# The five last pieces of the output, each stored as two sets of partitions

## The chip, the cores and the metric

The kernel runs on one core of one Trainium2 chip. A core has the engines TensorE (PE; its weight loads are listed apart, as PEld), VectorE (DVE), ScalarE (ACT), GpSimd (POOL) and SyncE (SP), and 16 DMA engines that move data between the chip's memory (HBM) and the core's on-chip memory (SBUF, 128 partitions). An instruction of SP, ACT or POOL can issue a DMA; the DMA engines then carry it out as packets, while the issuing engine goes on. The metric is the time of one execution on the device in microseconds (us), as the median of several runs. A profile is taken of one more execution; its span runs from the first to the last instruction of the program.

## The reference

Four batches of 6400 tokens with 256 channels. Attention runs over the channels (a 256 x 256 matrix for each batch), and its output goes through a mixture of eight low-rank adapters, of which each token takes two:

```
qn = q / (norm(q, axis=tokens) + 1e-6);  kn likewise        # q, k, v: 4 x 6400 x 256, f32
s  = kn^T @ qn / tau                                        # 4 x 256 x 256
a  = softmax(s, last axis)
x  = v @ a                                                  # 25600 x 256 rows
logits = x @ w_gate                                         # 8 experts
w  = softmax(the two largest logits of each row)
out = x + sum over the two experts e: w_e * ((x @ A[e]) @ B[e])   # A: 256x16, B: 16x256
```

The output is 25600 x 256 in f32, 26.2 MB.

## The kernel before, in words

**Layout.** Partition p of a batch holds the 50 tokens 50p to 50p+49 (`"(b p c) d -> b p c d"`), so a "chunk" c is one token of each of the 128 partitions: 128 rows of 256 numbers. Two chunks make a pair; there are 25 pairs in a batch (`NPAIR`) and 100 in all (`NPT`). In the output a pair is, on each partition, one stretch of 2 x 256 f32 numbers, that is 2 KB, and 256 KB over the 128 partitions.

**Stages.** For the first batch q and k are loaded, and their Gram matrix and the norms of their columns accumulate on TensorE. From then on each batch's v is worked on while the next batch's q and k come in. A pair goes through these steps: `transposes` (v turned round), `logits` and `gating` (per group of pairs), `z_gz` (the adapters' first half, times the gate), `y_mm` (v @ a), `gz_t` (transpose), `delta` (the adapters' second half added to y in the same accumulator, then the copy of the result to the SBUF tile `ys`, and its store).

**Groups and stores.** The pairs of a batch are bundled in groups of five that share one `ys` tile of 128 x 10 chunks (10 KB on a partition, 1280 KB in all); the last batch ends with groups of five, five, five, five, three and two. A group of five is stored whole by a DMA that ACT issues (`send`, line 666). The five last pairs of all (`u >= NPT - GRP` in `delta`, line 654: u = 95 to 99, the groups of three and two) are not stored by groups: each pair is stored by a DMA of its own that SP issues as soon as its copy to `ys` (line 651) is done (line 656). So the program has 19 stores from ACT and five from SP. SP does nothing else but to issue five loads at the very start (lines 206 to 213) and to wait at the end until all DMAs have landed (the waits stand under the last line of the launch, L886). Loads of q, k and v come from POOL (lines 181, 182, 185).

**What sets the order.** The order of the instructions is written by a planner in the Python code: it keeps an estimated clock for each engine and for the transfers and picks the next step that is ready. The five stores from SP aren't entered in these clocks. Each engine carries out its own instructions in the order of the program and waits at semaphores.

**Completion semaphores.** The framework below the kernel gives each DMA that SP or ACT issues one of eight completion semaphores, by turns, in the order of the program: the operands of these issues in the trace name 108, 109, 110, 111, 113, 116, 117, 118 and then 108 again, without a break from the first load to the last store. A DMA's landing counts that semaphore up, and in the trace the issuing engine waits, ahead of each of the five stores from SP, for the semaphore that the store is going to use, that is for the landing of the DMA eight places earlier in this sequence. The sequence ends as follows: the three last stores from ACT hold 116, 117 and 118, the five stores from SP hold 108, 109, 110, 111 and 113.

Of the kernel before, what the change touches and what calls it, by code (L numbers as in the profile page):

```python
# [16 lines left out]
def kernel(  # L17
# [16 lines left out]
    nc = tc.nc  # L34
# [11 lines left out]
    NPT = B * NPAIR  # L46
    GRP = 5
# [22 lines left out]
    def run(e, us, *deps):  # L70
        clock[e] = max([clock[e]] + [d + (0.0 if e == "pe" else 0.05) for d in deps]) + us
        return clock[e] + (0.2 if e == "pe" else 0.0)
# [35 lines left out]
    out_v = out.rearrange("(b p c) d -> b p c d", b=B, p=P)  # L108
# [334 lines left out]
    for b in range(B):  # L443
        f = 0
        for n in [5, 5, 5, 5, 3, 2] if b == B - 1 else [GRP] * (NPAIR // GRP):
            g = {"b": b, "f": b * NPAIR + f, "n": n, "ready": False}
            groups += [g] * n
            f += n
    pr = {}
    unsent = []  # L450
    free_from = [None]
# [185 lines left out]
    def delta(u):  # L637
        r, gr = pr[u], groups[u]
        for sc in range(2):
            nc.tensor.matmul(r["y"][:, sc, :], r["gzT"][:, sc, :], ball_sb, start=False,  # L640
                             stop=(sc == 1), skip_group_check=True)
        if "ys" not in gr:
            gr["ys"] = y_pool.tile([P, 2 * GRP, C], FP32, tag="ys", name="ys")
            ys_used.append(gr)
        dst = gr["ys"][:, r["w"]:r["w"] + 2, :]
        t_end = run("pe", 0.215)
        if clock["dve"] + 1.0 < clock["act"]:
            nc.vector.tensor_copy(dst, r["y"])
            r["y_end"] = run("dve", 0.69, t_end)
        else:  # L650
            nc.scalar.copy(dst, r["y"])  # L651
            r["y_end"] = run("act", 0.58, t_end)
        gr["y_end"] = r["y_end"]
        if u >= NPT - GRP:
            c0 = 2 * (u % NPAIR)
            nc.sync.dma_start(out_v[gr["b"], :, c0:c0 + 2, :], dst)
        elif u == gr["f"] + gr["n"] - 1:
            unsent.append(gr)

# [50 lines left out]
    while nd < NPT:  # L710
# [17 lines left out]
        while si["b"] < B and len(squared) < 4:  # L728
            b, c = si["b"], si["c"]
# [19 lines left out]
        if nl < len(order_g) and nt >= order_g[nl]["f"] + order_g[nl]["n"]:  # L749
            gr = order_g[nl]  # L750
# [3 lines left out]
        if nd < ny:  # L754
            r = pr[nd]
            gr = groups[nd]
# [33 lines left out]
        if gi["b"] < B:  # L790
            b, c = gi["b"], gi["c"]
# [31 lines left out]
        elif what == "delta":  # L823
            delta(nd)
            nd += 1
        elif what == "gzt":
            gz_t(ng)
            zuse_end[zuse_of[ng]] = pr[ng]["gzT_end"]
            ng += 1
        elif what == "y":  # L830
            y_mm(ny)
            ny += 1
        elif what == "z":
            if free_from[0] is None and chain_at[B - 1] >= 3:
                free_from[0] = nz
            zuse_of[nz] = zbank(nz)[0]
            z_gz(nz)
            nz += 1
        elif what == "t":
            transposes(nt)  # L840
            nt += 1
        elif what == "norm":
            norm()
        elif what == "gram":
            gram(gi["b"], gi["c"])
            gram(gi["b"], gi["c"] + 1)
            gi["c"] += 2
            if gi["c"] == NC:
                gi["b"], gi["c"] = gi["b"] + 1, 0
# [41 lines left out]
```

## Time and profile before

| what | value |
|---|---|
| time, median of 3 runs | 256.69 us (256.43 to 259.15) |
| time of the profiled execution | 256.61 us |
| its span, first to last instruction | 254.8 us |
| share of the span that engines are busy | PE 85%, PEld 76%, DVE 69%, ACT 63%, POOL 14% |
| mean granted TensorE clock | 0.969 of full speed |
| stores from ACT | 19 of 1280 KB, median 11.3 us from issue to landing |
| stores from SP | 5 of 256 KB, median 6.7 us from issue to landing |

The 1.8 us by which the execution is longer than its span lie before the first and after the last instruction. In a timeline, a row gives the start, the duration, the engine (SPq and ACTq are the sequencers that issue DMAs), the line of the kernel, the operation, and output<-input. In a table by windows, each row gives the stretch and its length, then busy time and number of instructions for each engine, the granted clock, the mean busy share of the 16 DMA engines (1.00: all 16 all the time) and the rate in GB/s. The list of DMA issues gives for each kind its number, its size and the median time from the issue to the landing of its last part.

### The profile page before, as it was taken

The page shows a single profiled execution, that of the slowest core. Times are in us where ns is not written, and L with a number is a line of the kernel's source. Part 1 is how long each engine was busy: PE and PEld are TensorE (multiplying, and loading weights), DVE is VectorE, ACT ScalarE, POOL GpSimd, SP SyncE. Part 2 cuts the span into 40 slices and gives each one's busy share as a digit, 9 for nine tenths or more (in the row PEclk, how much of TensorE's full clock was granted, in tenths as well). Part 3 has the DMA queues.
Part 4 walks back from the last instruction along what each step waited for, and adds up shares of the span by engine and source line. Part 5 has one row for each costly group of instructions (what it writes and reads, how often), then busy time and mean ns, then how long its engine had stood idle before and what let it go on. Part 6 is the DMA issues. An engine that isn't in the chain of part 4 may idle for free.

```text
span 254.8 us, 7166 instructions
## 1 busy us (share of the span) xinstructions
PE 216.9 (85%) x2972; PEld 193.0 (76%) x2972; DVE 174.9 (69%) x639; ACT 160.8 (63%) x289; POOL 36.3 (14%) x74
## 2 busy tenths in 40 slices
PE   1966996799999998999999887969877979999960
PEld 1755984599899997879888777868676869898840
DVE  1040006797979887688889878898657988887840
ACT  2000005688969889359799795958748847775550
POOL 7312341111121210200121010101000000000000
PEclk9998897999999999799999999999999999999995
DMA  7999999999999999999999999999999999999994
GB/s 212 226 214 212 209 216 212 216 215 212 216 214 213 217 213 213 216 214 227 302 257 272 279 252 299 228 316 238 292 241 287 264 265 330 394 425 422 428 411 193
DMA packets 13712, 66.79 MB, mean 262 GB/s; under 512 B 1648, under 2 KB 2416, under 8 KB 11248
## 3 DMA queue, kind: packets, MB, share of 16 engines
q0 software_dynamic: 9504, 38.80, 75.2%
q10 hardware_dynamic: 2736, 24.90, 23.6%
q1 hardware_dynamic: 1440, 2.63, 3.1%
q8 instruction: 23, 0.38, 0.5%
q14 instruction: 9, 0.07, 0.1%
HBM read 78.91 MB, written 26.21 MB: 413 GB/s over the span
## 4 chain that ended last, share of the span: by engine, by line
PE 50%; DMA 32%; DVE 6%; ACT 5%; issue 2%; POOL 1%; ACTq 1%; POOLq 0%
DMA qk<-in_k_dram 32%; PE y_ps L616 12%; PE acc L305 11%; PE vT_ps L467 6%; PE y_ps L640 6%; PE zg L599 5%; PE zg L625 3%; PE lp L495 3%; PE nrm L319 2%; ACT ys L651 2%; ACT sq L286 1%; PE nrm L330 1%; ACT vT L477 1%; POOL qk L181 1%; PE nrm L374 1%
## 5 line engine op out<-in xcount | busy, mean ns | idle before, releaser
L286 ACT ACTIVATE sq<-qk 128x1024 bf16<-128x1024 bf16 x69 | 69.6, 1056 | 4.9 <-DVE s L294 3.2
L305 PE MATMUL acc<-qk 128*128 128x256 bf16 x400 | 62.6, 284 | 4.3 <-DMA qk<-in_k_dram 4.3
L651 ACT COPY ys<-y_ps 128x512 f32<-128x512 f32 x94 | 53.4, 587 | 17.0 <-PE y_ps L640 16.6
L616 PE MATMUL y_ps<-a_bf,vT 128*128 128x256 bf16 x400 | 59.2, 272 | 2.4 <-ACT ys L651 2.2
L603 DVE TENSOR_TENSOR gz<-zg,gate 128x256 bf16<-128x256 f32 x100 | 41.2, 420 | 7.9 <-PE zg L599 7.1
L305 PEld LDWEIGHTS <-qk 128*128 128x128 bf16 x400 | 36.4, 101 | 8.1 <-DMA qk<-in_k_dram 4.8
L467 PE MATMUL vT_ps<-ident,vt 128*128 128x128 bf16 x400 | 36.6, 224 | 5.6 <-ACT vT L477 1.9
L616 PEld LDWEIGHTS <-vT 128*128 128x128 bf16 x400 | 35.9, 97 | 6.8 <-issue 3.5
L640 PE MATMUL y_ps<-ball_sb,gzT 128*128 128x256 bf16 x200 | 36.4, 273 | 1.7 <-ACT gzT L630 1.0
L599 PE MATMUL zg<-wa_sb,vT 128*128 128x128 bf16 x400 | 37.4, 219 | 0.0
L467 PEld LDWEIGHTS <-vt 128*128 128x128 bf16 x400 | 27.9, 101 | 8.7 <-issue 5.1
L294 DVE TENSOR_TENSOR s<-sq 128x512 bf16<-128x512 bf16 x75 | 30.4, 418 | 1.6 <-ACT sq L286 1.2
L319 PE MATMUL nrm<-qk 128*128 128x128 bf16 x200 | 22.3, 237 | 10.5 <-DVE qk L226 5.0
L477 ACT COPY vT<-vT_ps 128x512 bf16<-128x512 bf16 x38 | 22.2, 588 | 13.4 <-PE vT_ps L467 13.0
L480 DVE COPY vT<-vT_ps 128x512 bf16<-128x512 bf16 x62 | 25.1, 420 | 7.0 <-PE vT_ps L467 6.4
L599 PEld LDWEIGHTS <-vT 128*128 128x128 bf16 x400 | 27.4, 98 | 1.0 <-issue 0.2
L319 PEld LDWEIGHTS <-qk 128*128 128x128 bf16 x200 | 17.1, 107 | 13.4 <-DVE qk L226 5.0
L625 PE MATMUL zg<-ident,gz 128*128 128x128 bf16 x200 | 26.2, 219 | 0.8 <-DVE gz L603 0.8
L633 DVE COPY gzT<-zg 128x256 bf16<-128x256 bf16 x68 | 19.3, 288 | 7.2 <-PE zg L625 6.6
L181 POOL DMA_DIRECT2D qk<-in_q_dram x23 | 12.5, 543 | 63.9 <-ACT sq L286 25.4
L347 ACT ACTIVATE lnn<-ss 128x4 f32<-128x4 f32 x1 | 0.2, 205 | 32.5 <-DVE ss L346 32.5
L640 PEld LDWEIGHTS <-gzT 128*128 128x128 bf16 x200 | 16.6, 97 | 4.5 <-ACT gzT L630 1.7
(70 smaller groups left out, 227.2 us busy)
## 6 DMA issues: line engine op xcount, KB each, us to landing
out_dram<-ys ACTq DMA_DIRECT2D x19, 1280.0 KB, 11.3
vt<-in_v_dram POOLq DMA_DIRECT2D x20, 640.0 KB, 26.1
qk<-in_q_dram POOLq DMA_DIRECT2D x17, 640.0 KB, 24.0
qk<-in_k_dram POOLq DMA_DIRECT2D x17, 640.0 KB, 24.5
out_dram<-ys SPq DMA_DIRECT2D x5, 256.0 KB, 6.7
qk<-in_q_dram POOLq DMA_DIRECT2D x3, 320.0 KB, 19.7
qk<-in_k_dram POOLq DMA_DIRECT2D x3, 320.0 KB, 19.3
stage<-in_q_dram SPq DMA_DIRECT2D x1, 512.0 KB, 3.8
```

Of the source, the lines that this page charges most:

```text
L286: nc.scalar.activation(sq, x, ACT.Square)
L294: nc.vector.tensor_tensor(out=s2, in0=sq[:, :, 0, :], in1=sq[:, :, 1, :], op=OP.add)
L305: nc.tensor.matmul(acc[b][:, ic, :], t[:, 1, o, ic * P:(ic + 1) * P], t[:, 0, o, :], start=(c == 0 and ic == 0), stop=(c == NC - 1), skip_ ...
L319: nc.tensor.matmul(nrm[b][:, j * P:(j + 1) * P], x, x, start=(c == 0 and j == 0), stop=(c == NC - 1), skip_group_check=True)
L467: nc.tensor.matmul(pt[:, ic, sc * P:(sc + 1) * P], vt[:, o + sc, ic * P:(ic + 1) * P], ident, is_transpose=True, start=(i == 0), stop=(i = ...
L480: nc.vector.tensor_copy(dst, src)
L599: nc.tensor.matmul(z[:, sc, :], r["vT"][:, ic, sc, :], st[b]["wa"][:, ic, E:E + ER], start=(sc == 0 and ic == 0), stop=(sc == 1 and ic == ...
L603: nc.vector.tensor_tensor(out=gz.rearrange("p c (e r) -> p c e r", e=E), in0=z.rearrange("p c (e r) -> p c e r", e=E), in1=gr["gate"][:, r ...
L616: nc.tensor.matmul(y[:, sc, :], r["vT"][:, ic, sc, :], st[b]["a"][:, ic, :], start=(sc == 0 and ic == 0), stop=False, skip_group_check=True)
L625: nc.tensor.matmul(gt[:, sc, :], r["gz"][:, sc, :], ident, is_transpose=True, start=(sc == 0), stop=(sc == 1))
L640: nc.tensor.matmul(r["y"][:, sc, :], r["gzT"][:, sc, :], ball_sb, start=False, stop=(sc == 1), skip_group_check=True)
L651: nc.scalar.copy(dst, r["y"])
```

## The change

The store of each of the five last pairs, one DMA of 128 partitions before, is issued as two DMAs one after the other from SP for the first four pairs: partitions 0 to 119 and 120 to 127; 0 to 103 and 104 to 127; 0 to 87 and 88 to 127; 0 to 125 and 126 to 127. The fifth pair is stored by one DMA of 128 partitions as before. The bytes on each partition (2 KB) and their places in the output stay as they are. SP issues nine DMAs in place of five.

```diff
@@ -446,6 +446,7 @@
             g = {"b": b, "f": b * NPAIR + f, "n": n, "ready": False}
             groups += [g] * n
             f += n
+    ROWS = [[120, 128], [104, 128], [88, 128], [126, 128], [128]]
     pr = {}
     unsent = []
     free_from = [None]
@@ -653,7 +654,10 @@
         gr["y_end"] = r["y_end"]
         if u >= NPT - GRP:
             c0 = 2 * (u % NPAIR)
-            nc.sync.dma_start(out_v[gr["b"], :, c0:c0 + 2, :], dst)
+            lo = 0
+            for hi in ROWS[u - NPT + GRP]:
+                nc.sync.dma_start(out_v[gr["b"], lo:hi, c0:c0 + 2, :], dst[lo:hi])
+                lo = hi
         elif u == gr["f"] + gr["n"] - 1:
             unsent.append(gr)
```

## The prediction

> **What bounds the kernel now.** I read the page's chain of work first, then what goes on behind its end. The chain, in order of time, closes with the copy of the last pair:
>
> ```profile
> 247.43 0.59 ACT ys L651
> ```
>
> It ends at 248.02, but the span has 254.8 us. No compute engine works in the last 6.8 us; what runs are the DMA engines. The table by windows shows them (the column before the last is their mean busy share):
>
> ```profile
> 248.00:249.00 1.00, 0.00 (x0) 0.00 (x0) 0.00 (x0) 0.02 (x1) 0.00 (x0) 1.00 1.00 399
> 249.00:249.50 0.50, 0.00 (x0) 0.00 (x0) 0.00 (x0) 0.00 (x0) 0.00 (x0) 0.67 1.03 410
> 249.50:250.00 0.50, 0.00 (x0) 0.00 (x0) 0.00 (x0) 0.00 (x0) 0.00 (x0) 0.50 0.81 324
> 250.00:250.50 0.50, 0.00 (x0) 0.00 (x0) 0.00 (x0) 0.00 (x0) 0.00 (x0) 0.50 0.65 250
> 250.50:251.00 0.50, 0.00 (x0) 0.00 (x0) 0.00 (x0) 0.00 (x0) 0.00 (x0) 0.50 0.66 254
> 251.00:251.50 0.50, 0.00 (x0) 0.00 (x0) 0.00 (x0) 0.00 (x0) 0.00 (x0) 0.50 0.68 262
> 251.50:252.00 0.50, 0.00 (x0) 0.00 (x0) 0.00 (x0) 0.00 (x0) 0.00 (x0) 0.50 0.54 209
> 252.00:252.50 0.50, 0.00 (x0) 0.00 (x0) 0.00 (x0) 0.00 (x0) 0.00 (x0) 0.50 0.46 176
> 252.50:253.00 0.50, 0.00 (x0) 0.00 (x0) 0.00 (x0) 0.00 (x0) 0.00 (x0) 0.50 0.30 115
> 253.00:253.50 0.50, 0.00 (x0) 0.00 (x0) 0.00 (x0) 0.00 (x0) 0.00 (x0) 0.50 0.09 33
> ```
>
> A share times 16 is a number of engines: all 16 until 249.5, then 10 to 11 until 251.5 (0.65 to 0.68), 7 at 252.0 to 252.5, 5 after that, 1 or 2 at the end. So five or six engines are done by 250, and ten are **late**, the last of them by 3.5 us. From 248 on the shares add up to 1.00 + 0.5 x 5.22 = 3.61 us of all 16: spread evenly, the packets would end at 251.6. In fact the last two move after 253.3, as the queue's line of the window from 253.3 to the end has it:
>
> ```profile
> q1 hardware_dynamic: 2, 0.00, 0.4%
> ```
>
> So even a perfect spread is worth 253.4 - 251.6 = 1.8 us, 0.7% of the time.
>
> The timeline of ACT's two last stores and SP's five, and the list of issues for each of them in the same order, give issue and landing:
>
> ```profile
> 236.17 0.34 ACTq L666 DMA_DIRECT2D out_dram<-ys  x1
> 242.25 0.34 ACTq L666 DMA_DIRECT2D out_dram<-ys  x1
> 244.20 0.35 SPq L656 DMA_DIRECT2D out_dram<-ys  x1
> 244.69 1.01 SPq L656 DMA_DIRECT2D out_dram<-ys  x1
> 245.79 1.00 SPq L656 DMA_DIRECT2D out_dram<-ys  x1
> 246.89 0.58 SPq L656 DMA_DIRECT2D out_dram<-ys  x1
> 248.04 0.33 SPq L656 DMA_DIRECT2D out_dram<-ys  x1
> ```
>
> ```profile
> out_dram<-ys ACTq DMA_DIRECT2D x1, 1280.0 KB, 11.3
> out_dram<-ys ACTq DMA_DIRECT2D x1, 1280.0 KB, 8.7
> out_dram<-ys SPq DMA_DIRECT2D x1, 256.0 KB, 7.0
> out_dram<-ys SPq DMA_DIRECT2D x1, 256.0 KB, 7.1
> out_dram<-ys SPq DMA_DIRECT2D x1, 256.0 KB, 6.7
> out_dram<-ys SPq DMA_DIRECT2D x1, 256.0 KB, 6.2
> out_dram<-ys SPq DMA_DIRECT2D x1, 256.0 KB, 5.7
> ```
>
> The last store from ACT lands at 242.25 + 8.7 = 250.95, SP's first at 251.2, its third at 252.5, its fourth at 253.1, its fifth at 248.04 + 5.7 = 253.74, about 0.35 after the last packets. They land some 0.6 us apart although they are issued 0.5 to 1.2 apart: on the latest engine they stand in line. The span ends 1.1 us after the last landing.
>
> **The change part by part.** It removes four stores of 128 partitions, adds eight of fewer, all on SP's queue, and moves the fifth pair's store behind them. Nothing before 244.2 us can change: SP issues nothing there, and no other engine waits for these stores. Three things have to be costed.
>
> *Packets on the late engines.* The queue's line for the window from 240 us to the end:
>
> ```profile
> q1 hardware_dynamic: 720, 1.31, 21.4%
> ```
>
> 720 packets for five stores are 144 each: 128 rows of 2 KB and 16 completions, so eight rows on each of 16 engines, 40 in all. 21.4% of 16 engines over the 16 us asked for are 54.8 us, or 0.086 us for a row with its share of the completions; eight rows take 0.69 us, near the 0.6 by which the landings follow each other. What a set of 120 partitions does no row shows. By the nearest one (eight rows to an engine) 120 rows use 15 engines, 104 use 13, 88 use 11; 126 rows can go nine to an engine over 14. Then up to five engines are relieved, and the rest take 8 + 8 + 8 + 9 + 8 = 41 rows and their part of the small sets (8, 24, 40 and 2 rows): spread over all 16 that is 74 / 16 = 4.6 rows more, packed onto the same 8 to 12 engines up to 1 + 2 + 4 + 1 = 8. So a busiest engine has 46 to 49 rows in place of 40: **+0.5 to +0.8 us** if it is the latest one. Ten engines are late and at most five are relieved, so at least five late ones get more. At best the relieved ones are the five that end behind 252.5; then the next, packets ending by 252.5, get their 0.5 to 0.8 and land near 253.6: **-0.1**. Both ends are kept. The trace doesn't number the engines; I take +0.6, as an engine drawn from the late ones is more likely among the ten or eleven that get more.
>
> The Trainium skill (DMA: Bandwidth & Descriptors, "Why a DMA increments its semaphore by 16 and not by 1") says that a DMA from SP runs on the largest number of engines up to 16 that divides its slowest dimension, and takes the lowest-numbered. By that the nine stores use 15, 8, 13, 12, 11, 10, 14, 2 and 16 engines, engines 0 and 1 get 49 rows and engine 15 eight; the 16 completions of a 128-partition store agree with it, and no run so far shows the rest.
>
> *A new wait.* The page of waits for SP, and the rows of its line 656:
>
> ```profile
> SPq L656 <- DMA out_dram<-ys: 225.9, 1, 225.9
> SPq L656 <- ACT ys L651: 17.5, 4, 15.0
> SPq L886 <- DMA out_dram<-ys: 5.1, 5, 2.7
> ```
>
> ```profile
> L656 SPq EVENT_SEMAPHORE  x5: 17/17/17, 229.2 to 247.5; - x5
> L656 SPq DMA_DIRECT2D out_dram<-ys x5: 332/583/1011, 244.2 to 248.0; - x5
> ```
>
> Each store from SP has one wait of its own, and the first sat until an earlier store had landed, at 229.15. It is the 25th DMA of SP and ACT together, and the 17th was ACT's twelfth store:
>
> ```profile
> 217.04 0.34 ACTq L666 DMA_DIRECT2D out_dram<-ys  x1
> ```
>
> ```profile
> out_dram<-ys ACTq DMA_DIRECT2D x1, 1280.0 KB, 12.1
> ```
>
> 217.04 + 12.1 = 229.1: the wait is for the DMA eight places earlier, whose completion semaphore is used again. With five stores that costs nothing. With nine, the sixth waits for ACT's third last store, the seventh for the one of 236.17 (landed 247.5), the **eighth (two partitions) for ACT's last one, landed 250.95**, and the ninth for SP's own first (251.2 before). Behind the eighth stands the fifth pair's whole store. So in place of 248.04 it is issued at 250.95 + 0.09 (from a wait to the issue, as between 245.70 and 245.79) + 0.33 + 0.09 = 251.46; with an issue of 1.01 in place of 0.33, at 252.14. From an issue to the first packets it took 1.0 us at the empty start (the first load, and the queue up to 1.8; up to 1.7 it has none) and 2.0 to 2.1 beside full engines (the window from 244.2 to 246.3; up to 246.2 none):
>
> ```profile
> 0.74 0.37 SPq L206 DMA_DIRECT2D stage<-in_q_dram  x1
> ```
>
> ```profile
> q1 hardware_dynamic: 4, 0.02, 8.9%
> ...
> q1 hardware_dynamic: 3, 0.01, 0.8%
> ```
>
> At 251.5 half of the engines work; I take 1.5. With 0.69 of packets and 0.35 to the landing: 251.46 + 1.5 + 0.69 + 0.35 = **254.0**, bounds 253.5 (1.0) and 255.3 (252.14 + 2.1 + 0.69 + 0.4): -0.2 to +1.6 against 253.74. If ACT's store lands up to 0.69 sooner, because fewer of SP's rows run beside it on the latest engine, the wait for SP's own first keeps the issue from coming much sooner. A late engine isn't starved: with 33 to 41 rows to do before the last eight it is busy to 253.1 or beyond, and the fifth pair's rows arrive at 252.5 to 253.5.
>
> *Four more issues.* 0.33 to 1.01 us each. They lie between 244.2 and 251, where SP only waits: six issues from the second to the seventh at 1.01 + 0.09 end at 244.55 + 6.6 = 251.15, hardly behind the 250.95. They cost nothing unless every one is slow.
>
> The sum is the later of two paths, not their total: 253.74 + 0.6 = 254.35 by the late engines, 254.0 by the wait. **+0.6 us** on the profiled execution's 256.61 gives 257.2; the median is 0.1 above that execution, which I leave out.
>
> **The rivals.**
> *Relief hits.* The engines left out are the latest. For it: five engines do end behind 252.5. Against it: ten are late, and the wait puts the end at 253.5 or beyond. 253.5 in place of 253.74 is -0.2: 256.4.
> The Trainium skill (same page, "Rules for kernel authors") advises against splitting a transfer by partitions, because both parts use the same engines; that speaks against any relief, and no row yet shows it.
> *Rows stay where they were.* A set's rows go to the engines that the whole store gave them: the change shifts nothing, 40 rows each, and only the wait is left: 253.7 to 254.3, or 256.6 to 257.2. The 16 even shares speak neither way.
> *SP's queue.* Each issue takes the 1.01 of the slowest row: the eighth ends at 251.24 + 1.01, the ninth starts at 252.34 and lands at 254.4 to 255.5: 257.3 to 258.4. For it: two of five rows have 1.0. Against it: the last two have 0.58 and 0.33, when less was moving.
> *Few engines (slower).* The engines that carry a large set are the place: if one such set runs on one engine or a few, they become the bound. 120 rows on one are 112 more than now, 9.6 us; on a late engine that is 266, on one that is done 3.5 us early 263. The point from which it decides: 30 rows above the 40 on a late engine are 2.6 us, 1%. Against it: eight divides 120, 104 and 88, and nothing needs fewer engines; but all rows of before have 128 partitions.
>
> **How the numbers follow.** Forecast 0.48, relief 0.24, rows stay 0.10, SP's queue 0.10, few engines 0.07, something faster than the perfect spread 0.01. The first four lie between 256.3 and 258.4; with 0.2 for the runs' own spread below, the range is 256.1 to 258.5. A 1% step (2.6 us) is about what a measurement of this kernel can tell from no change: slower is few engines and a tail of SP's queue, 0.08; same holds the rest, 0.91; faster would need more than the 1.8 us of a perfect spread, 0.01.
>
> **What would show it.** In the profile after: the compute engines end at 248.0 as now; SP's ninth issue stands at 251 to 252.3, behind a wait for a store's landing; nine issues of 0.33 to 1.01; the busy share falls below 0.65 before 251 if engines are relieved, and the last landing is near 254.3. It is wrong if the ninth issue comes before 250 (no wait for the semaphore), if one set takes over 9 us to land, or if the shares stay at 0.65 to 251.5 (rows not shifted).

## The result, and the profile after

The changed kernel takes 257.42 us (median of 20 runs, 257.00 to 260.12) against 256.65 us (20 runs, 256.36 to 259.15): the ratio is 1.0038, with a 95% interval of 1.0021 to 1.0056. It is 0.5 to 1.4 us slower, so within 1%. The profiled execution took 257.15 us, with a span of 255.4, 0.54 longer than that of before.

The chain of work of the kernel after closes with the last copy again:

```profile
247.90 0.58 ACT ys L652
```

It ends at 248.48, 0.46 later than before. That doesn't explain the 0.54: the output still waiting in the queues hides a later copy (an experiment below has a copy that ended at 250.1 and no later landing), and ACT's last store, which the late engines had to finish first, has its last completion at 251.05, against 251.00 before. The table by windows of the kernel after, with the share of the DMA engines in the column before the last:

```profile
248.00:249.00 1.00, 0.00 (x0) 0.00 (x0) 0.00 (x0) 0.49 (x1) 0.00 (x0) 1.00 0.89 334
249.00:249.50 0.50, 0.00 (x0) 0.00 (x0) 0.00 (x0) 0.00 (x0) 0.00 (x0) 1.00 0.82 291
249.50:250.00 0.50, 0.00 (x0) 0.00 (x0) 0.00 (x0) 0.00 (x0) 0.00 (x0) 1.00 0.77 283
250.00:250.50 0.50, 0.00 (x0) 0.00 (x0) 0.00 (x0) 0.00 (x0) 0.00 (x0) 1.00 0.73 262
250.50:251.00 0.50, 0.00 (x0) 0.00 (x0) 0.00 (x0) 0.00 (x0) 0.00 (x0) 1.00 0.81 279
251.00:251.50 0.50, 0.00 (x0) 0.00 (x0) 0.00 (x0) 0.00 (x0) 0.00 (x0) 1.00 0.87 287
251.50:252.00 0.50, 0.00 (x0) 0.00 (x0) 0.00 (x0) 0.00 (x0) 0.00 (x0) 0.92 0.74 266
252.00:252.50 0.50, 0.00 (x0) 0.00 (x0) 0.00 (x0) 0.00 (x0) 0.00 (x0) 0.50 0.69 262
252.50:253.00 0.50, 0.00 (x0) 0.00 (x0) 0.00 (x0) 0.00 (x0) 0.00 (x0) 0.50 0.96 369
253.00:253.50 0.50, 0.00 (x0) 0.00 (x0) 0.00 (x0) 0.00 (x0) 0.00 (x0) 0.50 0.24 90
253.50:254.00 0.50, 0.00 (x0) 0.00 (x0) 0.00 (x0) 0.00 (x0) 0.00 (x0) 0.50 0.02 8
```

Before, the share fell from 249.5 on, with a level stretch near 0.66 until 251.5, as one engine after the other ran out. Now it falls from 248 to 0.73 at 250.0, goes up to 0.87 and down to 0.69 until 252.5, and then rises to 0.96: nearly all 16 engines work at once on a store that comes late. In the rows of SP's stores (line 659 now), in its waits, and in the timeline and the list of issues for the last store, one can see which:

```profile
L659 SPq DMA_DIRECT2D out_dram<-ys x9: 236/618/1137, 244.7 to 251.4; - x9
L659 SPq EVENT_SEMAPHORE  x5: 17/17/17, 228.9 to 251.3; - x5
```

```profile
SPq L659 <- DMA out_dram<-ys: 226.5, 2, 225.7
...
SPq L890 <- DMA out_dram<-ys: 2.2, 1, 2.2
```

```profile
249.85 0.43 SPq L659 DMA_DIRECT2D out_dram<-ys  x1
251.06 0.24 SPq L659 DMA_DIRECT2D out_dram<-ys  x1
251.40 0.36 SPq L659 DMA_DIRECT2D out_dram<-ys  x1
```

```profile
out_dram<-ys SPq DMA_DIRECT2D x1, 256.0 KB, 2.6
```

SP now waits twice for the landing of a store: 225.7 us for the first, as before, and 226.5 - 225.7 = 0.8 us for another. The seventh issue ends at 250.28, the eighth (two partitions) starts at 251.06, just after ACT's last store has landed at 251.05, and the ninth, the fifth pair's whole store, follows at 251.40, after SP's own first store has landed at 251.21. It lands at 254.03 (before 253.74). The end is longer as well: from the last landing to the end of the span it was 254.82 - 253.74 = 1.08 us before, and it is 255.37 - 254.03 = 1.33 us after. So the 0.54 are 0.29 of a later landing and 0.25 of a longer end.

The trace also records the single completions of a store, 16 for one of 128 partitions; I read each as the last of one DMA engine's share. Counted and timed for the kernel after, in us (not a view of the profile; after the first time of a row only what changes is written, and the middle is left out):

```
store        completions  landings: the first six, the last four
ACT's last        16      247.05 .08 .19 .24 .32 .46 ... 250.52 250.56 250.71 251.05
120 rows          15      248.00 .11 .20 .32 .39 249.21 ... 250.79 250.83 250.93 251.21
8                  8      248.29 .37 .38 .53 249.93 250.11 250.38 251.00
104               13      248.83 .91 249.07 .45 .75 250.46 ... 251.48 251.54 251.57 251.84
24                12      249.09 .25 .34 .62 .95 250.65 ... 251.58 251.66 251.74 251.75
88                11      250.30 .44 .61 .72 .81 251.26 ... 251.71 252.21 252.29 252.34
40                10      251.04 .13 .25 .43 .46 .56 ... 251.79 252.03 252.54 252.66
126               14      252.08 .13 .16 .17 .20 .45 ... 252.84 253.03 253.27 253.38
2                  2      252.44 252.49
128               16      253.24 .26 .28 .30 .32 .34 ... 253.65 253.66 253.90 254.03
```

The counts agree in every row with the rule of the Trainium skill (DMA: Bandwidth & Descriptors, "Why a DMA increments its semaphore by 16 and not by 1"): the largest number of engines up to 16 that divides the partitions. With the rule's second half, that the lowest-numbered ones are taken (which no run here shows by itself), the rows also tell who was late. ACT's last store has six early engines and ten late ones; the set of 120 has five early and ten late, so the engine it leaves out (15) was an **early** one. The set of 104 still has five early and eight late, the one of 24 five and seven, the one of 88 five and six: the engines left out there were late ones, the very latest (251.84, missing in the set of 24) among them. Two late engines are in every set of ten or more and land last, at 253.90 and 254.03; 14 of 16 have landed by 253.66. These two are never short of work at the end: taking the two last of a row for the same two engines, the fourth pair's rows land there at 253.27 and 253.38, and the fifth pair's some 0.64 later, about the 0.69 that eight rows take.

### The profile page after: what moved, and what is told of

It is laid out like the page before. It is cut to its first block, busy times and chain, and to the rows that moved or that the text cites. A ratio compares the mean times of both kernels' runs of the same rounds, so it can differ in the third digit from the quotient of the medians.

```text
span 255.4 us, 7170 instructions
## 1 busy us (share of the span) xinstructions
PE 219.5 (86%) x2972; PEld 194.9 (76%) x2972; DVE 174.8 (68%) x639; ACT 160.6 (63%) x289; POOL 36.3 (14%) x74
## 4 chain that ended last, share of the span: by engine, by line
PE 43%; DMA 38%; ACT 6%; DVE 5%; issue 4%; POOL 0%; ACTq 0%; POOLq 0%; DVEq 0%
DMA vt<-in_v_dram 18%; PE y_ps L617 12%; DMA qk<-in_q_dram 10%; DMA qk<-in_k_dram 10%; PE vT_ps L468 7%; PE acc L305 6%; PE y_ps L641 6%; PE zg L600 5%; PE lp L496 3%; PE zg L626 3%; ACT ys L652 2%; ACT sq L286 2%; ACT vT L478 1%; PE nrm L330 1%; PE nrm L374 1%
## 5 line engine op out<-in xcount | busy, mean ns | idle before, releaser
L617 PE MATMUL y_ps<-a_bf,vT 128*128 128x256 bf16 x400 | 60.1, 275 | 2.7 <-ACT ys L652 2.3
L617 PEld LDWEIGHTS <-vT 128*128 128x128 bf16 x400 | 36.4, 98 | 7.5 <-issue 3.9
L641 PE MATMUL y_ps<-ball_sb,gzT 128*128 128x256 bf16 x200 | 37.0, 276 | 1.7 <-ACT gzT L631 1.0
L600 PE MATMUL zg<-wa_sb,vT 128*128 128x128 bf16 x400 | 38.3, 222 | 0.0
L600 PEld LDWEIGHTS <-vT 128*128 128x128 bf16 x400 | 28.0, 99 | 1.1 <-issue 0.2
L185 POOL DMA_DIRECT2D vt<-in_v_dram x20 | 10.6, 530 | 64.6 <-DMA qk<-in_q_dram 15.7
```

The lines of the kernel that those rows point to most:

```text
L600: nc.tensor.matmul(z[:, sc, :], r["vT"][:, ic, sc, :], st[b]["wa"][:, ic, E:E + ER], start=(sc == 0 and ic == 0), stop=(sc == 1 and ic == ...
L617: nc.tensor.matmul(y[:, sc, :], r["vT"][:, ic, sc, :], st[b]["a"][:, ic, :], start=(sc == 0 and ic == 0), stop=False, skip_group_check=True)
```

## The experiments

All start from the changed kernel unless said otherwise; times of before were measured beside each kernel, so they differ a little. Two theories stand against each other: **the wait** (the fifth pair's store is late, because its issue stands behind a wait for a semaphore) and **the shifted rows** (late engines get more rows than they had).

### Nine stores with equal rows on all engines

```diff
-    ROWS = [[120, 128], [104, 128], [88, 128], [126, 128], [128]]
+    ROWS = [[112, 128], [112, 128], [112, 128], [112, 128], [128]]
```

> All four split pairs as 112 and 16 partitions: nine stores as in the change, but both sets divide by 16, so that every engine should keep its eight rows of a pair. What is left of the change is the number of stores: the wait of the eighth and ninth for a semaphore, four more issues, and the order of the waits at the end. If the wait is what makes the change slower: the ninth issue at 251.0 to 251.6, the busy share low at 251.5 to 252.5 and near 1 after it, last landing 253.7 to 254.1, time 0.3 to 0.8 us over before. If the shifted rows are: the late engines have 40 rows as before and are never short of work, last landing 253.7, time at most 0.3 us over before.

Measured: 257.30 against 256.52 us, ratio 1.0031 (1.0007 to 1.0055). Every store has 16 completions. The ninth issue and its landing:

```profile
251.36 0.37 SPq L659 DMA_DIRECT2D out_dram<-ys  x1
```

```profile
out_dram<-ys SPq DMA_DIRECT2D x1, 256.0 KB, 2.5
```

The last completion came at 253.85, and the span ended at 255.18, again 1.33 later. So with no row shifted the late issue stays and so does the longer end; the landing is 0.11 later than before, in place of 0.29. Of the 255.37 - 254.82 = 0.55 us by which the change's span is longer, 0.36 don't need the uneven sets, 0.25 of them the longer end.

### The same sets, the small ones behind the whole store

```diff
+    later = []
 ...
-            lo = 0
-            for hi in ROWS[u - NPT + GRP]:
-                nc.sync.dma_start(out_v[gr["b"], lo:hi, c0:c0 + 2, :], dst[lo:hi])
-                lo = hi
+            hi = ROWS[u - NPT + GRP][0]
+            nc.sync.dma_start(out_v[gr["b"], 0:hi, c0:c0 + 2, :], dst[0:hi])
+            if hi < 128:
+                later.append((out_v[gr["b"], hi:128, c0:c0 + 2, :], dst[hi:128]))
+            else:
+                for o, i in later:
+                    nc.sync.dma_start(o, i)
```

> The same sets as in the change, but the four small ones (8, 24, 40 and 2 partitions) are issued after the fifth pair's whole store. The whole store is then the fifth from SP and finds its semaphore free; the two last small sets (40 and 2 rows) take the waits. If the wait of the whole store is the cost: it is issued near 249, the engines that are done early get its rows early, last landing 253.5 or sooner, time 0.3 to 0.6 us under the change and within 0.3 of before. If the shifted rows are the cost: the latest engines have as many rows as in the change, last landing 254.0 or later, time within 0.2 us of the change.

Measured: 257.01 against 256.52 us, ratio 1.0018 (0.9997 to 1.0038). The whole store is issued 1.6 us sooner:

```profile
249.78 0.41 SPq L659 DMA_DIRECT2D out_dram<-ys  x1
```

```profile
out_dram<-ys SPq DMA_DIRECT2D x1, 256.0 KB, 3.6
```

It lands at 253.36. But now the set of 40, issued at 251.31, lands last, at 253.97, and the span ends at 255.15, 1.18 later. SP's waits for a landing are one, the early one that before has too:

```profile
SPq L659 <- DMA out_dram<-ys: 225.9, 1, 225.9
```

The two landings that could have held the sets of 40 and 2, of ACT's last store (250.93) and SP's first (251.32), came while SP was still issuing other sets; each issue starts 0.05 after the one ahead of it ends. So no store waited for a late landing here, the rows are shifted as in the change, and the last landing hardly moved: 253.97 for 254.03, about the 254.0 expected of shifted rows, and not the 253.5 or sooner expected of the wait. For the landing this run speaks for the shifted rows. The time lies between the two expectations (0.49 us over before, the change 0.77).

### The small sets from GpSimd

```diff
-                nc.sync.dma_start(out_v[gr["b"], lo:hi, c0:c0 + 2, :], dst[lo:hi])
+                e = nc.gpsimd if lo else nc.sync
+                e.dma_start(out_v[gr["b"], lo:hi, c0:c0 + 2, :], dst[lo:hi])
```

> The same sets, but the four small ones are issued from GpSimd, which has completion semaphores of its own: SP has its five stores of before and no wait for a landing among them. If the wait is the cost: the fifth store is issued by 249, time within 0.3 us of before. If the shifted rows are: time 0.4 us or more over before, with the fifth store issued by 249. If the four issues are: SP has only five, so time as before.

Measured: 260.43 (six runs) against 256.52 us, ratio 1.0121 (1.0088 to 1.0154), worse than every expectation. In its profile the last copy ends only at 252.25, and the granted clock of TensorE (the third column from the right) was low in two stretches in which it was 1.00 before:

```profile
195.00:200.00 5.00, 5.00 (x64) 4.30 (x63) 2.85 (x9) 3.62 (x6) 0.00 (x0) 0.77 1.05 231
205.00:210.00 5.00, 3.55 (x34) 2.80 (x34) 4.04 (x19) 2.27 (x5) 0.00 (x0) 0.76 1.03 287
```

The span also ends 2.1 us after the last landing (258.50 against 256.39). Why the compute is late isn't settled: nothing was issued differently before 248 us. As a test of the wait it is **inconclusive**, because the fifth store was now held by its copy (issued at 252.27).

### One set on one engine

```diff
+    ROWS = [[127, 128], [128], [128], [128], [128]]
```

> One pair alone split, into 127 partitions and 1; six stores. If a set runs on the largest number of engines that divides its partitions, 127 rows stand on one engine: 127 x 0.084 = 10.7 us of packets behind a start at 246.3, and that engine's rows of the other stores beside them, so last landing 258 to 262 and 5 to 8 us over before. If rows are dealt eight to an engine: last landing within 0.3 us of before.

Measured: 264.73 us in one run, 8.2 over the 256.52 of before and so a little more than the 5 to 8 expected. The set of 127 and that of one partition have a single completion each. The windows at the end:

```profile
254.00:256.00 2.00, 0.00 (x0) 0.00 (x0) 0.00 (x0) 0.00 (x0) 0.00 (x0) 0.50 0.46 166
256.00:258.00 2.00, 0.00 (x0) 0.00 (x0) 0.00 (x0) 0.00 (x0) 0.00 (x0) 0.50 0.07 26
258.00:260.00 2.00, 0.00 (x0) 0.00 (x0) 0.00 (x0) 0.00 (x0) 0.00 (x0) 0.50 0.07 26
```

A share of 0.07 is one engine of 16, from 256 to the last landing at 261.9. So the rival "few engines" describes something that happens, at about the price it was given. It doesn't apply to the change, whose four large sets ran on 11 to 15 engines.

### Seven stores, equal rows; eight stores, equal rows

```diff
+    ROWS = [[112, 128], [112, 128], [128], [128], [128]]      # seven
+    ROWS = [[112, 128], [112, 128], [112, 128], [128], [128]] # eight
```

> Two pairs split into 112 and 16 partitions, seven stores from SP: equal rows on every engine, no store behind a wait for a late landing (the seventh waits for a store that lands near 247.5). If more issues and more sets by themselves cost something, the last landing moves beyond 253.9; if only the late wait, the shifted rows and the order of the last waits do, it stays at 253.6 to 253.8, and the span ends about 0.95 us after it (one wait behind it in place of three), time within 0.2 us of before.

> Three pairs split into 112 and 16 partitions, eight stores from SP: the fifth pair's whole store is the eighth and waits for ACT's last store (250.9 to 251.0), but nothing waits for SP's own first one, and its semaphore is the last in the order of the waits at the end. If the late wait alone costs time: whole store issued at 251.0 to 251.1, last landing 253.5 to 253.9, most of the 16 shares landing within 0.5 us of each other. If the order of the last waits is a cost of its own: the span ends 0.9 us after the last landing, not 1.33 as in the change, and the time is within 0.2 us of before.

Measured: seven, 256.76 against 256.50 us, ratio 1.0030 (0.9998 to 1.0061); eight, 256.28 against 256.50, ratio 0.9994 (0.9971 to 1.0017). The last store of the eight:

```profile
251.00 0.35 SPq L659 DMA_DIRECT2D out_dram<-ys  x1
```

```profile
out_dram<-ys SPq DMA_DIRECT2D x1, 256.0 KB, 2.7
```

It is issued at 251.00, held by ACT's last store like the eighth in the change, yet it lands at 253.71, as before (253.74), since a late engine is then still busy with the rows of the fourth pair (landed at 253.07). **In this profile the wait until 251.0 alone costs nothing.** The end took 0.90 us, and 0.97 with seven stores (last landing 253.59). The time of the one with seven misses its expectation, at 0.26 us over before in place of at most 0.2; its landing and its end are those expected.

The one with seven shows the cover that the prediction didn't count on. Its last copy came 2.1 us later than before in the profiled execution (chain of work):

```profile
249.53 0.58 ACT ys L652
```

and still it landed 0.15 earlier. It also shows that the issues aren't free on SP itself: the last store is issued at 251.10, 1.0 us after its copy ended at 250.11, with no landing to wait for, only other issues of 0.36 to 1.13 us ahead of it.

The kernel with eight stores was measured a second time:

> The kernel with three pairs split into 112 and 16 partitions once more, in more rounds: if its eighth store's wait is free and only the order of the last waits differs from before, 0.1 to 0.3 us under before; if the wait costs, 0.2 us or more over it.

Measured: 256.68 against 256.41 us, ratio 1.0031 (1.0007 to 1.0055), with a last landing at 253.85 and an end of 0.91. By its expectation the time (0.27 us over before) says that the wait costs; the first measurement (0.22 under) says that it doesn't. The same kernel thus gave 0.9994 and 1.0031. Two ratios that differ by 0.3% don't rank these kernels; what ranks them here are the landings and the ends in the profiles, each from one execution, and the landings of these two profiles differ by 0.14.

### Shifted rows without a late wait

```diff
+    ROWS = [[88, 128], [88, 128], [128], [128], [128]]
```

> Two pairs split into 88 and 40 partitions, seven stores, no late wait. By the counts of engines 11 and 10 ten engines get 24 rows for these two pairs in place of 16, five get none of them and one 16. If shifted rows cost time: an engine that is late and gets eight rows more ends 0.5 to 0.7 us later, last landing 254.0 to 254.4, time 0.1 to 0.5 us over before. If the five without rows are the latest and the ten have slack: last landing 253.5 or sooner and the time 0.2 us or more under before.

Measured: 256.86 against 256.50 us, ratio 1.0041 (1.0005 to 1.0076). Seven stores, the last issued before the 251.0 of the wait:

```profile
250.60 0.56 SPq L659 DMA_DIRECT2D out_dram<-ys  x1
```

```profile
out_dram<-ys SPq DMA_DIRECT2D x1, 256.0 KB, 3.4
```

The last completions are at 253.60, 253.72, 253.88 and 254.02; with equal rows and the same number of stores they were at 253.54, 253.55, 253.55 and 253.59. In both kernels the last copy came some 2 us later than in the kernel before (250.03 and 250.11), so they can be compared with each other. The shift does cost time here: 254.02 - 253.59 = 0.43. That the last four are late engines with eight rows more is an inference; the trace doesn't number the engines.

### The order of the last waits

At the end SP waits for the eight semaphores one after the other, always in the same order, 108 first and 118 last (with the loads below, the eight are 108 to 111, 113, 114, 116 and 117). In the change the last store holds 108, in the kernel before 113. Three small loads more turn the semaphores on by three:

```diff
     nc.sync.dma_start(bst, moe_B.rearrange("e r d -> (e r) d"))
+    spare = const.tile([P, 3, CC * E], FP32, name="spare")
+    for i in range(3):
+        nc.sync.dma_start(spare[:, i, :], moe_w_gate.rearrange("(p cc) e -> p (cc e)", p=P))
```

> The change with three more small loads from SP at the start (8 KB each, of data that nothing uses), which turn the semaphores on by three: the sets, their waits for the DMA eight places earlier and the loads of the engines are those of the change, but the last store's semaphore is the fourth in the order of the waits at the end, not the first. If that order is part of the cost: the span ends 1.10 to 1.20 us after the last landing in place of 1.33, and the time is about 0.2 us under the change. If not: 1.33 and the time of the change.

> The kernel before with three more small loads from SP at the start (8 KB each, nothing uses them) and nothing else: the five last stores are whole, and the semaphore of the last one is the last in the order of the waits at the end. If that order has a price of its own: last landing at 253.5 to 253.9 as in the kernel before, the span ends 0.9 us after it in place of 1.08, time 0.1 to 0.3 us under before. If not: 1.08 and the time of before.

Measured: in the changed kernel 257.14 against 256.50 us, ratio 1.0043 (1.0008 to 1.0079), lowest run 0.62 over that of before, where the change's is 0.64 over it; in the kernel before 256.57 against 256.41, ratio 1.0003 (0.9985 to 1.0021). The last store of each, changed kernel first, then before:

```profile
251.34 0.36 SPq L662 DMA_DIRECT2D out_dram<-ys  x1
```

```profile
out_dram<-ys SPq DMA_DIRECT2D x1, 256.0 KB, 2.8
```

```profile
248.68 0.33 SPq L659 DMA_DIRECT2D out_dram<-ys  x1
```

```profile
out_dram<-ys SPq DMA_DIRECT2D x1, 256.0 KB, 5.0
```

The landings stay (254.10 and 253.65), the ends shrink as expected: 255.24 - 254.10 = 1.14 for 1.33, and 254.55 - 253.65 = 0.90 for 1.08. The trace shows the waits 0.06 us apart (in the change they start at 254.05, 254.11, 254.17 and so on to 254.48): seven stand behind the last landing in the change, four in this version of it, three before, none in this version of before. With 0.90 for none, that gives 1.32, 1.14 and 1.08, within 0.01 of what was measured, and 0.96 for the one that stands behind it in the kernels with seven stores (0.97). With the small sets last, the semaphore that is waited for first belongs to the set of two, which landed at 253.80, and 253.80 + 1.33 = 255.13 is where that span ends (255.15), not 0.9 after the last landing. So the longer end is shown in the profiles; that the time of the whole falls with it isn't: the changed kernel gains nothing in its lowest run, and the second kernel's expected gain of 0.1 to 0.3 lies within its interval without showing in the median.

### The readings side by side

All from the profiled executions; the end is the span after the last landing.

| kernel | last copy ends | last issue | last landing | end | span |
|---|---|---|---|---|---|
| before | 248.02 | 248.04 | 253.74 | 1.08 | 254.82 |
| changed | 248.48 | 251.40 | 254.03 | 1.33 | 255.37 |
| nine, equal rows | 249.24 | 251.36 | 253.85 | 1.33 | 255.18 |
| small sets last | 249.66 | 251.69 | 253.97 | 1.18 | 255.15 |
| changed, semaphores turned | 248.23 | 251.34 | 254.10 | 1.14 | 255.24 |
| seven, 88 and 40 | 250.03 | 250.60 | 254.02 | 0.97 | 254.99 |
| eight, equal rows | 248.28 | 251.00 | 253.71 | 0.90 | 254.61 |
| eight, again | 248.91 | 251.06 | 253.85 | 0.91 | 254.76 |
| seven, equal rows | 250.11 | 251.10 | 253.59 | 0.97 | 254.56 |
| before, semaphores turned | 248.66 | 248.68 | 253.65 | 0.90 | 254.55 |

Kernels with shifted rows land at 253.97 to 254.10, those with equal rows at 253.59 to 253.85, on the mean 0.30 apart and without overlap. Neither the last copy nor the last issue orders the landings: with equal rows they lie within 0.26 us for last issues from 248.04 to 251.36. None was shown to beat the kernel before.

## Why the prediction was right, point by point

**The size and sign hold:** +0.6 us was forecast on the profiled execution, +0.54 measured; 257.2 forecast, 257.42 the median, inside the range. But one term of the sum was too large and another was left out, and that the two errors nearly cancel is luck.

*Packets on the late engines: the mechanism right, the term mis-sized.* Forecast +0.5 to +0.8 on the latest engine, a landing at 254.35; measured 254.03, +0.29. The engine that was latest up to the set of 104 is one of those relieved (it has no rows of the sets of 24, 88 and 40), and what ends last are two engines that were somewhat less late and take more rows. So the rival "relief hits" was right that the latest engine is relieved, but not on the end, because other late engines get its rows, as the forecast had it. The rival "rows stay where they were" falls by the counts of completions, the rival "relief hits" by the later landing. The price of the shift is 0.30 between the means of the table, 0.43 between the two kernels with seven stores.

*The new wait: right in place and time, not in price.* Forecast issue of the ninth store 251.46, measured 251.40, behind the landing forecast at 250.95 and measured at 251.05. Its landing by this path alone was put at 254.0; it didn't set the end, because the two last engines still had rows of the fourth pair to do until 253.38, and with the same rows and no such wait (small sets last) the landing was 253.97. 14 of the 16 engines had finished by 253.66, and 253.85 is where the nine equal stores end. The 1.5 us from the issue to the first packets, taken midway between 1.0 and 2.0, were too long: the first completion at 253.24, less 0.35 and the 0.69 of eight rows, leaves some 0.8. With equal rows a wait until 251.0 moved the landing by -0.03 and +0.11 (eight stores, two profiles), one until 251.4 by +0.11: no cost that stands out from the spread.

*Four more issues: right.* They moved no landing, though one took 1.14 us, more than the slowest row of before; the seventh ended at 250.28, 0.8 ahead of the wait's end. The rival "SP's queue" had it end at 251.15 and the ninth start at 252.34.

*The end: the step that failed.* "The span ends 1.1 us after the last landing" was carried over as a constant. It is 1.33 in the change, because nine stores turn the semaphores on by four and the last store's is then waited for first, with seven waits to go through behind it. These 0.25 make up for the 0.3 that the late engines' term had too much.

*Two signs that failed.* A share below 0.65 before 251 was to show that engines are relieved, and a share that stays at 0.65 until 251.5 that rows aren't shifted. It was 0.73 to 0.87 from 250.0 to 251.5, neither of the two. The mean share of 16 engines didn't settle where the rows went; the completions did. And the last copy was to end at 248.0 as before; it ended at 248.48, and the first store from SP was issued at 244.67, 0.47 later.

*Few engines: right to leave it at a small chance.* The sets had 15, 8, 13, 12, 11, 10, 14 and 2 completions; only the sets of 127 and of one partition, in the experiment, had one.

What stays open is the rest of the difference in the medians, 0.77 against the 0.54 of the two profiles (the interval has 0.5 to 1.4 us); why the late engines were late; and the late compute of the kernel that stores from GpSimd.

## What to carry to other kernels

Count the DMAs that wait for each other's completion semaphores before splitting a store: with eight semaphores in turn, the ninth store in a row waits for the first, and whatever stands behind it in the queue waits too. Here a backlog of rows covered that wait. A spread over DMA engines can be steered by the number of partitions, but leaving out a late engine isn't enough: its rows go to others, and here two other late engines got them and ended later. The completions of one store by all engines, set beside those of a smaller set, help to tell which are late. Where the end of a kernel is a backlog of stores, look at what comes behind the last landing as well: it isn't a constant.

## What was not expected of the hardware

Sixteen engines with equal rows end 3.8 us apart (the fifth store of before: first completion at 249.93, last at 253.74), six early and ten late. The trace doesn't tell why.

A copy that is 2 us late leaves the end where it was: in the kernel with seven equal stores the 16 engines took the last store almost together (253.40 to 253.59), and the lateness was gone.

An issue from SP can take several us: in the kernel with 127 partitions on one engine, the issue right behind that store took 5.6 us, against at most 1.0 to 1.5 in the other kernels. What held it the trace doesn't tell; it ended at 250.9, long before that store landed at 259.3.

```profile
L659 SPq DMA_DIRECT2D out_dram<-ys x6: 324/449/5593, 244.9 to 252.8; - x6
```
